# Converting float64 weights on Trainium2: the exponent handled by ScalarE's copy instead of a second VectorE mask

## The chip, the cores and the metric

The kernel runs on one core of one Trainium2 chip. Its time is the device time of one execution in microseconds (us), taken as the median of several runs. The engines are TensorE (PE in the profile; its weight loads are PEld), VectorE (DVE), ScalarE (ACT), GpSimd (POOL) and SyncE (SP), which issues the DMAs here.

## The reference

Attention with queries pooled in pairs, then two MLPs one after the other. The four MLP weight matrices arrive as float64, everything else as float32.

```python
# q, k, v: (4, 8, 1152, 64) float32; weights float64: w_in (512, 2048), w_out (2048, 512)
q_pool = q.reshape(B, H, S // 2, 2, D).mean(axis=3)
scores = q_pool @ k.T / sqrt(D)
attn = softmax(scores) @ v                 # per batch and head: 576 queries, 1152 keys
x = attn, heads side by side               # (2304, 512)
h = x @ moe_w_in;  x = maximum(0.01 * h, h) @ moe_w_out
h = x @ moe2_w_in; x = where(h > 0, h, exp(min(h, 0)) - 1) @ moe2_w_out
```

## The kernel before

All matrix products are done as sums of "high" and "low" float32r parts, so each operand is split: ScalarE or VectorE rounds the high part, GpSimd or VectorE subtracts it from the operand (`psplit`, L261 to L267). A source line that is such a helper's stands for many tiles, so the tile names matter: `wi` and `wo` are the split weights, `g` the split MLP activations, `pt` the split attention weights, `kn`, `qn`, `vn` the split inputs.

The work is cut into 16 attention pairs (a batch and two heads; nine query tiles each) and eight MLP passes (four batches, two layers). Attention of batch 1 runs beside the MLPs of batch 0, and so on; the MLPs of batch 3 run alone at the end. A pair ends with the normalising transposes L535. This document counts pairs from 0, so pairs 4 to 7 are batch 1.

The order of instructions on every engine is written out ahead of time. `Program.add` takes each operation with an engine, a planned cost and a rank; `Program.schedule` simulates all engines with those costs and sorts the operations by their planned start. Every engine, SyncE's DMA queue too, then takes its own list strictly in order. An edit of one operation therefore moves others, on all engines.

An MLP pass works through 16 slices of 128 hidden columns (`up`, L638; `down`, L676), in halves of 288 rows; one half of one slice is 12 matmuls in `up`, and a block of four slices for one output tile 12 in `down`. Layer 0's activation is finished on VectorE at L651, layer 1's at L659, and `down`'s partial sums are added at L689. On first use a weight slice is read as float64 and converted by `convert`, called from `load_w`; the float32 result is split at once and also stored to DRAM (L328), from where the later batches load it. `convert` runs 128 times over a chunk of 256 columns: 2 layers x 16 slices x 2 matrices x 2 chunks. Its buffers are rings of two (`CB`): `cr` holds the raw words, low and high interleaved, `ct` the word under construction, `cm` a second copy. A chunk's load (L290) can only start when the chunk two before it has left `cr`.

Per chunk, before: VectorE shifts the high word left by three and masks it (L293), VectorE puts the two top bits in (L296), ScalarE scales the low word (L299) and takes the magnitude of the high word (L301), GpSimd adds low to high (L303), and VectorE zeroes what is below float32's range (L305).

Of the kernel before, what the change touches and what calls it, by code (L numbers as in the profile page):

```python
# [9 lines left out]
F32 = mybir.dt.float32  # L10
F32R = mybir.dt.float32r
U32 = mybir.dt.uint32
ACTF = mybir.ActivationFunctionType
ALU = mybir.AluOpType
# [140 lines left out]
def kernel(  # L155
# [20 lines left out]
    V, A, G, PE = nc.vector, nc.scalar, nc.gpsimd, nc.tensor  # L176
# [10 lines left out]
    FT = DFF // 128  # L187
    QSCALE = 0.5 / float(D) ** 0.5
    HB = NQ // 2
    MIN_HI = 2.0 ** (112 - 127) * (1 + 2.0 ** -3)  # L190
    PTB = 4
    CW = 256
    CB = 2
# [47 lines left out]
    prog = Program()  # L241

    def sb(tag, shape, dt=F32, bufs=1):
        return prog.buf(tag, bufs, lambda: sp.tile(shape, dt, tag=tag, name=tag, bufs=bufs))
# [4 lines left out]
    def act(n, accum=False, sbuf=False):  # L249
        return 50 + 0.833 * n + (190 if accum else 0) + (43 if sbuf else 0)  # L250

    def dve(n, fast=False):
        return 66 + (0.52 if fast else 1.05) * n

    def pool(n):
        return 140 + 2.12 * n
# [14 lines left out]
    def convert(rank, dst, src):  # L271

        for n in range(0, 512, CW):
            r = sb("cr", [128, CW, 2], U32, CB)
            t = sb("ct", [128, CW], U32, CB)  # L280
            mag = sb("cm", [128, CW], F32, CB)

            def load(n=n, r=r):
                rv = r.ap.rearrange("p n t -> p (n t)")
                if len(src.shape) == 3:
                    k0, kn = n // src.shape[2], CW // src.shape[2]
                    rv, sv = rv.rearrange("p (c n) -> p c n", c=kn), src[:, k0:k0 + kn, :]
                else:
                    sv = src[:, n:n + CW]
                nc.sync.dma_start(out=rv, in_=sv.bitcast(U32))  # L290

            prog.add("SP", 60, rank - 1, load, w=[r])
            prog.add("DVE", dve(CW, True), rank, lambda r=r, t=t: V.tensor_scalar(  # L293
                out=t.ap, in0=r[:, :, 1], scalar1=3, scalar2=0x3FFFFFF8,
                op0=ALU.logical_shift_left, op1=ALU.bitwise_and), w=[t], r=[(r, 1)])
            prog.add("DVE", dve(CW), rank, lambda r=r, t=t: V.scalar_tensor_tensor(  # L296
                out=t.ap, in0=r[:, :, 1], scalar=0xC0000000, in1=t.ap,
                op0=ALU.bitwise_and, op1=ALU.bitwise_or), w=[t], r=[(r, 1), t])
            prog.add("ACT", act(CW, sbuf=True), rank, lambda r=r: A.activation(  # L299
                out=r[:, :, 0], in_=r[:, :, 0], func=ACTF.Copy, scale=2.0 ** -29), w=[(r, 0)], r=[(r, 0)])  # L300
            prog.add("ACT", act(CW, sbuf=True), rank, lambda r=r, mag=mag: A.activation(  # L301
                out=mag.ap, in_=r[:, :, 1].bitcast(F32), func=ACTF.Abs), w=[mag], r=[(r, 1)])
            prog.add("POOL", pool(CW), rank, lambda t=t, r=r: G.tensor_tensor(  # L303
                out=t.ap, in0=t.ap, in1=r[:, :, 0], op=ALU.add), w=[t], r=[t, (r, 0)])
            prog.add("DVE", dve(CW), rank, lambda n=n, t=t, mag=mag: V.scalar_tensor_tensor(  # L305
                out=dst[:, n:n + CW], in0=mag.ap, scalar=MIN_HI, in1=t.ap.bitcast(F32),
                op0=ALU.is_ge, op1=ALU.mult), w=[(dst, n)], r=[t, mag])

    kept = {}

    def load_w(rank, layer, w_in, w_out, f, mine):

        src = (w_in[:, f * 128:(f + 1) * 128].rearrange("(c p) f -> p c f", p=128),
               w_out[f * 128:(f + 1) * 128, :])
        rs = [mine("wr", [128, 512], F32, WRB, "p", PBUF) for _ in range(2)]
        for i, r in enumerate(rs):
            if w_in.dtype == F32:
                view = (lambda r=r: r.ap.rearrange("p (c n) -> p c n", c=DC)) if i == 0 else lambda r=r: r.ap
                prog.add("SP", 60, rank - 1.5, lambda i=i, view=view: nc.sync.dma_start(
                    out=view(), in_=src[i]), w=[r])  # L320
            elif (layer, f, i) in kept:
                kp = kept[layer, f, i]
                prog.add("SP", 60, rank - 1.5, lambda r=r, kp=kp: nc.sync.dma_start(
                    out=r.ap, in_=kp.ap), w=[r], r=[kp])
            else:
                convert(rank - CLEAD, r, src[i])
                kp = kept[layer, f, i] = Buf(lambda i=i: dram.tile([128, 512], F32, name=f"w{layer}_{f}_{i}"))
                prog.add("SP", 60, rank, lambda r=r, kp=kp: nc.sync.dma_start(out=kp.ap, in_=r.ap), w=[kp], r=[r])  # L328
        wi = mine("wi", [128, 2, DC, 128], F32R, WIB, "qT", KTB)
        wo = mine("wo", [128, 2, DM], F32R, WOB, "kT", KTB)  # L330
        psplit(rank - 0.5, WH, WL, lambda: wi[:, 0].rearrange("p c n -> p (c n)"),
               lambda: wi[:, 1].rearrange("p c n -> p (c n)"), lambda: rs[0].ap, 512, (wi, 0), [rs[0]])
        psplit(rank - 0.5, WH, WL, lambda: wo[:, 0], lambda: wo[:, 1], lambda: rs[1].ap, 512, (wo, 0), [rs[1]])
        return wi, wo
# [3 lines left out]
    for j in range(2):  # L338
        t = sp.tile([128, 2, 128], F32R, name=f"rem{j}")
# [400 lines left out]
    for b, layer, at, wide in PLAN:  # L740
        tags = [(u, size[u]) for u in ("h" * HBUFS + ("t" * TB + "s" * SBUFS if wide else ""))]
        w = ((moe_w_in, moe_w_out), (moe2_w_in, moe2_w_out))[layer]
# [35 lines left out]
```

## Time and profile before

| | |
|---|---|
| median of 3 runs | 1539.69 us (1537.06 to 1542.2) |
| profiled execution | span 1538.0 us from the first to the last instruction; no other time is recorded for it |
| PE busy | 1414.5 us, 92% |
| PEld busy | 1365.5 us, 89% |
| ACT busy | 1065.2 us, 69% |
| DVE busy | 1011.8 us, 66% |
| POOL busy | 829.8 us, 54% |
| mean granted TensorE clock | 0.988 |

Busy shares are means over stages that differ: the conversions all lie in the first 592 us, where VectorE is far busier than in the mean. They are therefore read stretch by stretch below.

### The profile page before, as it was taken

The numbers are of one execution on the slowest core, as the hardware profiler recorded it, in microseconds if no ns is written. First come the engines' busy times: TensorE is split into PE (matmuls) and PEld (weight loads), VectorE is DVE, ScalarE is ACT, GpSimd is POOL, SyncE is SP. The second block draws the span as 40 slices with busy tenths as digits, with TensorE's granted clock in tenths as the row PEclk, the third lists the DMA queues.
The fourth block names the chain that finished last, engine by engine and source line by source line (L and its number), as shares of the span: only waits on it lengthen the run. The fifth ranks groups of instructions, "written<-read, shape, count | busy, mean of one in ns | idle before, by whom it ended". The sixth has DMA issues, their size and how long they took to land.

```text
span 1538.0 us, 28928 instructions
## 1 busy us (share of the span) xinstructions
PE 1414.5 (92%) x10288; PEld 1365.5 (89%) x10288; DVE 1011.8 (66%) x2273; ACT 1065.2 (69%) x2901; POOL 829.8 (54%) x840
## 2 busy tenths in 40 slices
PE   5877889988888898999999999999999999999998
PEld 4777788888778887999999999899999998899998
DVE  6999888899998998556665556556665454123222
ACT  6998878776688787676668777676667773443553
POOL 5443355765766667354555555255555445466661
PEclk9999999999999999999999999999999999999999
DMA  4232123344434443222222222222222222323210
GB/s 147 91 115 87 40 77 121 122 130 129 127 119 139 132 143 118 76 75 69 69 68 86 79 78 64 71 71 61 76 71 64 56 63 63 106 77 89 70 55 32
DMA packets 82642, 135.59 MB, mean 88 GB/s; under 512 B 8512, under 2 KB 26944, under 8 KB 82496
## 3 DMA queue, kind: packets, MB, share of 16 engines
q1 hardware_dynamic: 82496, 133.73, 28.5%
q8 instruction: 81, 1.33, 0.4%
q14 instruction: 65, 0.53, 0.1%
HBM read 112.20 MB, written 21.50 MB: 87 GB/s over the span
## 4 chain that ended last, share of the span: by engine, by line
PE 63%; DVE 20%; ACT 7%; DMA 4%; issue 3%; POOL 2%; SPq 0%; ACTq 0%; POOLq 0%; DVEq 0%
PE h L676 16%; PE h L638 16%; PE s L452 8%; PE o L496 7%; PE t L475 5%; DVE m L457 3%; DVE ct L293 3%; DVE wr L305 3%; PE s L638 3%; PE s L676 3%; DVE ct L296 2%; DVE pt L267 2%; PE t L638 2%; PE t L373 2%; PE t L676 2%
## 5 line engine op out<-in xcount | busy, mean ns | idle before, releaser
L676 PE MATMUL h<-g,wo 128*128 128x288 f32 x2460 | 425.8, 303 | 16.7 <-DVE t L659 7.9
L638 PE MATMUL h<-xs,wi 128*128 128x288 f32 x2448 | 418.1, 305 | 23.3 <-DVE t L659 13.5
L638 PEld LDWEIGHTS h<-xs,wi 128*128 128x128 f32 x2448 | 351.8, 190 | 33.1 <-DVE t L659 19.0
L676 PEld LDWEIGHTS h<-g,wo 128*128 128x128 f32 x2460 | 356.9, 189 | 23.1 <-DVE t L659 9.9
L457 DVE TENSOR_REDUCE m<-s 128x1 f32<-128x384 f32 x432 | 231.8, 550 | 71.9 <-PE s L452 68.9
L261 ACT ACTIVATE pt<-t 128x384 fp32r<-128x384 f32 (+2 forms) x426 | 188.0, 456 | 117.3 <-PE t L475 109.1
L463 ACT ACTIVATE p<-s,m 128x384 f32<-128x384 f32 x432 | 249.1, 587 | 19.1 <-DVE m L459 18.7
L267 DVE TENSOR_TENSOR pt<-t,pt 128x384 fp32r<-128x384 f32 (+1 forms) x416 | 206.6, 508 | 74.0 <-ACT pt L261 72.6
L452 PE MATMUL s<-kT,qT 128*128 128x384 f32 x768 | 198.5, 356 | 25.7 <-ACT p L463 25.0
L267 POOL TENSOR_TENSOR g<-t,g 128x288 fp32r<-128x288 f32 x216 | 179.1, 833 | 67.6 <-ACT g L261 62.4
L267 POOL TENSOR_TENSOR wo<-wr,wo 128x512 fp32r<-128x512 f32 x112 | 145.9, 1307 | 108.2 <-ACT wo L261 106.3
L496 PE MATMUL o<-pt,vn 128*128 128x256 f32 (+1 forms) x1152 | 192.1, 302 | 5.4 <-DVE pt L267 3.5
L475 PE MATMUL t<-ident,p 128*128 128x128 f32 x1116 | 181.8, 277 | 12.3 <-DVE pt L267 11.3
L267 POOL TENSOR_TENSOR wi<-wr,wi 128x512 fp32r<-128x512 f32 x110 | 144.0, 1310 | 62.9 <-ACT wi L261 48.9
L496 PEld LDWEIGHTS o<-pt,vn 128*128 128x128 f32 x1152 | 165.1, 190 | 10.4 <-DVE pt L267 10.0
L475 PEld LDWEIGHTS t<-ident,p 128*128 128x128 f32 x1116 | 139.8, 142 | 21.9 <-DVE pt L267 11.8
L452 PEld LDWEIGHTS s<-kT,qT 128*128 128x128 f32 x768 | 126.2, 193 | 32.9 <-ACT p L463 31.8
L303 POOL TENSOR_TENSOR ct<-ct,cr 128x256 uint32<-128x256 uint32 x128 | 98.8, 774 | 95.5 <-DVE ct L296 33.8
L267 POOL TENSOR_TENSOR vn<-raw,vn 128x576 fp32r<-128x576 f32 x32 | 46.3, 1448 | 174.5 <-ACT vn L261 174.5
L261 ACT ACTIVATE g<-t 128x288 fp32r<-128x288 f32 x216 | 95.9, 446 | 44.1 <-DVE t L659 26.2
L689 DVE TENSOR_TENSOR acc<-h,acc 128x288 f32<-128x288 f32 x158 | 71.0, 452 | 66.2 <-PE h L676 64.9
L261 ACT ACTIVATE wo<-wr 128x512 fp32r<-128x512 f32 x112 | 70.5, 630 | 46.3 <-PE h L676 33.5
(150 smaller groups left out, 2228.4 us busy)
## 6 DMA issues: line engine op xcount, KB each, us to landing
wr<-w SPq DMA_DIRECT2D x172, 256.0 KB, 2.7
cr<-in_moe_w_in_dram SPq DMA_DIRECT2D x64, 256.0 KB, 2.8
cr<-in_moe_w_out_dram SPq DMA_DIRECT2D x64, 256.0 KB, 2.7
w<-wr SPq DMA_DIRECT2D x64, 256.0 KB, 2.4
raw<-in_k_dram SPq DMA_DIRECT2D x32, 288.0 KB, 3.0
raw<-in_v_dram SPq DMA_DIRECT2D x32, 288.0 KB, 3.1
raw<-in_q_dram SPq DMA_DIRECT2D x32, 256.0 KB, 2.9
p<-w SPq DMA_DIRECT2D x20, 256.0 KB, 2.6
```

The lines of the kernel that those rows point to most:

```text
L261: prog.add("ACT", act(n, sbuf=not psum), rank, lambda: A.activation(out=hi(), in_=src(), func=ACTF.Copy), w=[w], r=r)
L267: lambda: eng.tensor_tensor(out=lo(), in0=src(), in1=f32(hi()), op=ALU.subtract),
L293: prog.add("DVE", dve(CW, True), rank, lambda r=r, t=t: V.tensor_scalar(out=t.ap, in0=r[:, :, 1], scalar1=3, scalar2=0x3FFFFFF8, op0=ALU.l ...
L303: prog.add("POOL", pool(CW), rank, lambda t=t, r=r: G.tensor_tensor(out=t.ap, in0=t.ap, in1=r[:, :, 0], op=ALU.add), w=[t], r=[t, (r, 0)])
L452: PE.matmul(out=st[:, 0:384], lhsT=qa(a), rhs=kT[:, 384 * c:384 * c + 384], start=(i == 0), stop=(i == len(seq) - 1))
L457: prog.add("DVE", dve(384), rank - LR, lambda st=st, c=c: V.tensor_reduce(out=m[:, c:c + 1], in_=st[:, 0:384], axis=AX.X, op=ALU.max), w=[ ...
L463: prog.add("ACT", act(384, True), rank - LE, lambda c=c: A.activation(out=p[:, 384 * c:384 * c + 384], in_=banks[c][:, 0:384], func=ACTF.E ...
L475: PE.transpose(out=t[:, i, :], in_=p[:, (3 * c + i) * 128:(3 * c + i + 1) * 128], identity=ident)
L496: PE.matmul(out=o[:, 0:n], lhsT=vn[:, c, :], rhs=pt[th][:, a, c % 3, :], start=(c == 3 * ORDER[0] and a == 0), stop=(c == 3 * ORDER[2] + 2 ...
L638: PE.matmul(out=h[:, 0:HB], lhsT=wi[:, a, c, :], rhs=xs[c][:, e, cols], start=(c == 0 and a == 0 and e == 0), stop=(c == DC - 1 and a == 1))
L676: PE.matmul(out=y[:, 0:HB], lhsT=w[f][1][:, a, d * 128:(d + 1) * 128], rhs=g[f][:, e, cols], start=(f % FC == 0 and a == 0 and e == 0), st ...
L689: prog.add("DVE", dve(HB), rank - HURRY, lambda y=y, a_=a_, cols=cols: V.tensor_tensor(out=a_[:, cols], in0=y[:, 0:HB], in1=a_[:, cols], o ...
```

## The change

ScalarE copies the high word, read as a float32, with a scale of 2^-112, which rebases the exponent in the arithmetic and sends what is too small to zero, into `cm`. VectorE shifts that copy left by three (one operation, contiguous input), GpSimd adds the low part as before, and VectorE joins the sign bit of the copy to the sum. The second VectorE mask (L296) and the magnitude copy (L301) are gone; the comparison at L305 becomes a bitwise join. Per chunk there are two ScalarE, two VectorE and one GpSimd instruction where there were two, three and one. The shift now reads what ScalarE wrote, where L293 read the loaded word itself.

```diff
-            mag = sb("cm", [128, CW], F32, CB)
+            g = sb("cm", [128, CW], F32, CB)
...
-            prog.add("DVE", dve(CW, True), rank, lambda r=r, t=t: V.tensor_scalar(
-                out=t.ap, in0=r[:, :, 1], scalar1=3, scalar2=0x3FFFFFF8,
-                op0=ALU.logical_shift_left, op1=ALU.bitwise_and), w=[t], r=[(r, 1)])
-            prog.add("DVE", dve(CW), rank, lambda r=r, t=t: V.scalar_tensor_tensor(
-                out=t.ap, in0=r[:, :, 1], scalar=0xC0000000, in1=t.ap,
-                op0=ALU.bitwise_and, op1=ALU.bitwise_or), w=[t], r=[(r, 1), t])
+            prog.add("ACT", act(CW, sbuf=True), rank, lambda r=r, g=g: A.activation(
+                out=g.ap, in_=r[:, :, 1].bitcast(F32), func=ACTF.Copy, scale=REBIAS), w=[g], r=[(r, 1)])
             prog.add("ACT", act(CW, sbuf=True), rank, lambda r=r: A.activation(
                 out=r[:, :, 0], in_=r[:, :, 0], func=ACTF.Copy, scale=2.0 ** -29), w=[(r, 0)], r=[(r, 0)])
-            prog.add("ACT", act(CW, sbuf=True), rank, lambda r=r, mag=mag: A.activation(
-                out=mag.ap, in_=r[:, :, 1].bitcast(F32), func=ACTF.Abs), w=[mag], r=[(r, 1)])
+            prog.add("DVE", dve(CW, True), rank, lambda g=g, t=t: V.tensor_scalar(
+                out=t.ap, in0=g.ap.bitcast(U32), scalar1=3, scalar2=None,
+                op0=ALU.logical_shift_left), w=[t], r=[g])
             prog.add("POOL", pool(CW), rank, lambda t=t, r=r: G.tensor_tensor(
                 out=t.ap, in0=t.ap, in1=r[:, :, 0], op=ALU.add), w=[t], r=[t, (r, 0)])
-            prog.add("DVE", dve(CW), rank, lambda n=n, t=t, mag=mag: V.scalar_tensor_tensor(
-                out=dst[:, n:n + CW], in0=mag.ap, scalar=MIN_HI, in1=t.ap.bitcast(F32),
-                op0=ALU.is_ge, op1=ALU.mult), w=[(dst, n)], r=[t, mag])
+            prog.add("DVE", dve(CW), rank, lambda n=n, t=t, g=g: V.scalar_tensor_tensor(
+                out=dst[:, n:n + CW].bitcast(U32), in0=g.ap.bitcast(U32), scalar=0x80000000, in1=t.ap,
+                op0=ALU.bitwise_and, op1=ALU.bitwise_or), w=[(dst, n)], r=[t, g])
```

In the changed kernel the ScalarE copies are L293 (high) and L295 (low), the shift is L297, the GpSimd add L300, the join L302; all lines behind are three lower (L457 becomes L454).

VectorE's order in pair 5, around the pair's remainder tile (`pt` of 3x64), before. L457 is the row maximum of the scores, L651 layer 0's activation:

```order
L267 TENSOR_TENSOR pt<-t,pt 128x3x64
L457 TENSOR_REDUCE m<-s 128x1
L305 SCALAR_TENSOR_TENSOR wr<-cm,ct 128x256
L267 TENSOR_TENSOR pt<-t,pt 128x3x64
L293 TENSOR_SCALAR ct<-cr 128x256
L296 SCALAR_TENSOR_TENSOR ct<-cr,ct 128x256
L651 TENSOR_TENSOR t_4545<-h,t_4545 128x288
L457 TENSOR_REDUCE m<-s 128x1
L305 SCALAR_TENSOR_TENSOR wr<-cm,ct 128x256
```

The same place in the changed kernel (L454 is the row maximum, L648 the activation):

```order
L297 TENSOR_SCALAR ct<-cm 128x256
L454 TENSOR_REDUCE m<-s 128x1
L297 TENSOR_SCALAR ct<-cm 128x256
L456 TENSOR_REDUCE m<-m 128x1
L267 TENSOR_TENSOR pt<-t,pt 128x3x64 x3
L648 TENSOR_TENSOR t_4503<-h,t_4503 128x288
L454 TENSOR_REDUCE m<-s 128x1
L648 TENSOR_TENSOR t_4514<-h,t_4514 128x288
L454 TENSOR_REDUCE m<-s 128x1 x2
L302 SCALAR_TENSOR_TENSOR wr<-cm,ct 128x256 x2
```

Two chunks now go through side by side: two shifts, other work, two joins; a row maximum stands behind each shift, where before it stood behind the activation or the join.

ScalarE's order there, before (L261 with `pt`, `g`, `wi`: high parts; L463 the softmax exponential, L649 the activation's first half):

```order
L261 ACTIVATE pt<-t 128x3x64
L649 ACTIVATE t_4491<-h 128x288
L463 ACTIVATE p,sum<-s,m 128x384 x2
L261 ACTIVATE g<-t_4491 128x288
L261 ACTIVATE pt<-t 128x3x64
L299 ACTIVATE cr<-cr 128x256
L301 ACTIVATE cm<-cr 128x256
L649 ACTIVATE t_4545<-h 128x288
```

And in the changed kernel (L646 is the activation, L460 the exponential):

```order
L646 ACTIVATE t_4428<-h 128x288
L261 ACTIVATE pt<-t 128x3x64 x2
L293 ACTIVATE cm<-cr 128x256
L295 ACTIVATE cr<-cr 128x256
L261 ACTIVATE g<-t_4428 128x288
L293 ACTIVATE cm<-cr 128x256
L295 ACTIVATE cr<-cr 128x256
L261 ACTIVATE wo<-wr 128x512
L460 ACTIVATE p,sum<-s,m 128x384 x3
```

The copy of the high word now comes first of a chunk's two, and in these rows two chunks stand close together with one split of `g` between them.

## Rows read from the trace of the kernel before

**Rows 1.** The page, part 1: busy time and share of the span.

```profile
PE 1414.5 (92%) x10288; PEld 1365.5 (89%) x10288; DVE 1011.8 (66%) x2273; ACT 1065.2 (69%) x2901; POOL 829.8 (54%) x840
```

**Rows 2.** Windows, busy us (instructions) of each engine; boundaries are the pairs' L535.

```profile
core 0: us, PE busy (x) PEld busy (x) DVE busy (x) ACT busy (x) POOL busy (x), PEclk, DMA share, GB/s
65.00:112.00 47.00, 38.04 (x262) 34.49 (x261) 43.87 (x109) 42.75 (x123) 21.24 (x22) 0.96 0.32 100
...
158.00:201.00 43.00, 35.65 (x258) 32.57 (x257) 36.03 (x88) 36.41 (x105) 12.04 (x13) 1.00 0.14 42
201.00:270.00 69.00, 63.24 (x445) 59.06 (x443) 60.25 (x141) 56.31 (x162) 37.39 (x39) 0.98 0.33 103
...
270.00:589.00 319.00, 278.97 (x1968) 260.61 (x1966) 300.70 (x629) 243.11 (x681) 212.59 (x223) 0.99 0.42 131
...
589.00:679.00 90.00, 81.82 (x595) 79.51 (x594) 55.59 (x124) 62.27 (x167) 43.51 (x43) 0.96 0.28 84
...
679.00:933.00 254.00, 253.49 (x1924) 252.41 (x1923) 151.44 (x352) 180.43 (x491) 133.65 (x130) 1.00 0.25 72
...
933.00:1027.00 94.00, 89.02 (x648) 86.66 (x647) 55.06 (x121) 63.61 (x172) 47.06 (x46) 0.96 0.25 77
...
1450.00:1500.00 50.00, 50.00 (x379) 50.00 (x378) 12.35 (x29) 26.90 (x65) 32.53 (x32) 1.00 0.20 61
```

**Rows 3.** The same windows, L638 alone, then L676 alone: PE, PEld.

```profile
679.00:933.00 254.00, 98.55 (x576) 81.96 (x576) 1.00 0.25 72
...
679.00:933.00 254.00, 101.73 (x585) 85.37 (x585) 1.00 0.25 72
```

**Rows 4.** The chain that ended last, in 270 to 589 us, by line.

```profile
by line: DVE ct L293 10.5%; DVE wr L305 10.4%; DVE ct L296 9.8%; issue 7.9%; DVE m L457 7.1%; DVE pt L267 5.5%; DMA cr<-in_moe_w_out_dram 5.3%; PE h L638 4.4%; DMA cr<-in_moe_w_in_dram 3.3%; DVE acc L689 3.1%; ACT p L463 3.0%; POOL ct L303 
```

**Rows 5.** Groups of VectorE by line, 270 to 589 us: busy us, mean ns | idle before.

```profile
L305 DVE SCALAR_TENSOR_TENSOR wr<-cm,ct 128x256 f32<-128x256 f32 x90 | 63.6, 710 | 1.3 <-POOL ct L303 1.2
L296 DVE SCALAR_TENSOR_TENSOR ct<-cr,ct 128x256 uint32<-128x256 uint32 x90 | 59.7, 665 | 0.7
L293 DVE TENSOR_SCALAR ct<-cr 128x256 uint32<-128x256 uint32 x90 | 51.2, 571 | 1.6 <-DMA cr<-in_moe_w_out_dram 0.9 <-DMA cr<-in_moe_w_in_dram 0.6
...
L689 DVE TENSOR_TENSOR acc<-h,acc 128x288 f32<-128x288 f32 x40 | 17.8, 447 | 2.0 <-PE h L676 1.9
```

**Rows 6.** Tile `ct`, whole run: ns min/median/max, then idle until (us, times).

```profile
L293 DVE TENSOR_SCALAR ct<-cr x128: 272/294/1524, 7.8 to 587.7; 128x256 uint32<-128x256 uint32 x128
L296 DVE SCALAR_TENSOR_TENSOR ct<-cr,ct x128: 403/425/1659, 9.4 to 589.2; 128x256 uint32<-128x256 uint32 x128
L303 POOL TENSOR_TENSOR ct<-ct,cr x128: 729/747/1034, 11.9 to 589.7; 128x256 uint32<-128x256 uint32 x128
L305 DVE SCALAR_TENSOR_TENSOR wr<-cm,ct x128: 402/416/1678, 12.7 to 591.4; 128x256 f32<-128x256 f32 x128
...
  DVE ct L296: 33.8, 26
...
  ACT cr L299: 6.2, 5
```

**Rows 7.** Timeline at 286 us: start us, duration us, instruction.

```profile
286.68 1.49 POOL L267 TENSOR_TENSOR wo<-wr,wo 128x512 fp32r<-128x512 f32 x1
...
286.94 1.38 DVE L293 TENSOR_SCALAR ct<-cr 128x256 uint32<-128x256 uint32 x1
...
288.13 0.85 POOL L267 TENSOR_TENSOR g<-t,g 128x288 fp32r<-128x288 f32 x1
...
288.36 0.91 DVE L296 SCALAR_TENSOR_TENSOR ct<-cr,ct 128x256 uint32<-128x256 uint32 x1
```

**Rows 8.** Tile `cr`, whole run: ScalarE's two copies.

```profile
L299 ACT ACTIVATE cr<-cr x128: 418/438/489, 7.8 to 587.4; 128x256 uint32<-128x256 uint32 x128
...
L301 ACT ACTIVATE cm<-cr x128: 414/428/478, 8.1 to 588.0; 128x256 f32<-128x256 f32 x128
```

**Rows 9.** Tile `qs`: a contiguous VectorE tensor_scalar of the same size.

```profile
L399 DVE TENSOR_SCALAR qs<-qs x32: 229/286/1494, 8.6 to 1141.4; 128x256 f32<-128x256 f32 x32
```

**Rows 10.** Waits of the DMA queue, 201 to 589 us: us, times, longest.

```profile
SPq L290 <- POOL ct L303: 156.4, 101, 5.2
```

**Rows 11.** Waits of VectorE, 270 to 589 us: us, times, longest.

```profile
DVE t L651 <- ACT t L649: 4.4, 4, 2.7
```

More of the change, by code (lines that the diff above doesn't have):

```diff
@@ L189 @@
     HB = NQ // 2
-    MIN_HI = 2.0 ** (112 - 127) * (1 + 2.0 ** -3)
+    REBIAS = 2.0 ** -112
     PTB = 4
```

## Prediction

> **What bounds the kernel now.** I read the page's busy shares first [rows 1]: TensorE is busy 92% of the span, so at first sight it bounds everything and VectorE, at 66%, nothing. Then I cut the span at the ends of the attention pairs [rows 2]. From 679 to 933 us (pairs 9 to 11, no conversions) TensorE is busy 253.5 of 254 us: bound by TensorE, and nothing on VectorE can help. From 270 to 589 us (pairs 5 to 7, where 90 of the 128 chunks are converted) it is the other way round: VectorE is busy 300.7 of 319 us, 94.3%, TensorE 279, ScalarE 243, GpSimd 213. There VectorE is the bound, and the chain of waits of that stretch says so: L293, L305 and L296 are its three longest lines, 30.7% of it together [rows 4].
>
> How much could come back at most? In 1450 to 1500 us only MLP matmuls run, 379 in 50 us without a gap [rows 2]: 0.132 us each. Pairs 9 to 11 hold 576 + 585 = 1161 of them [rows 3], 153 us, which leaves 33.6 us of TensorE for the attention of one pair. The order of before puts 1197 MLP matmuls into pairs 5 to 7, so TensorE alone would need 3 x 33.6 + 1197 x 0.132 = 259 us. They take 319. The conversions cost 60 us here; that is the room.
>
> **The change, part by part.** *The mask L296 goes.* Alone it takes 0.41 us (shortest 403 ns, median 425); in pairs 5 to 7 its mean is 665 ns [rows 5, 6]. The difference is waiting, and the timeline shows for what [rows 7]: GpSimd subtracts for `wo` from 286.68 to 288.17; the shift that VectorE starts at 286.94 lasts until 288.32, 1.38 us instead of 0.28. The mask behind it starts at 288.36, under the next GpSimd instruction, and takes 0.91. So the relief per chunk lies between 0.41 us (the waiting passes to the next instruction in line) and 0.665 us (it leaves too): 37 to 60 us in 90 chunks. I take 0.41, because the two instructions that stay, shift and join, meet the same GpSimd. [...]
>
> *The shift* reads contiguous words instead of every second one. L399, contiguous and as large, has 229 ns at its shortest and 286 at its median, against 272 and 294 for L293 [rows 6, 9]: between 0 and 43 ns less, at most 4 us in 90 chunks. I take 0, as the medians agree. [...]
>
> *The join* is a two-input bitwise instruction like L296, 403 ns at its shortest, for a comparison of 402 [rows 6]: nothing. *ScalarE* does two copies per chunk as before; a scaled copy (median 438) for a magnitude (428) [rows 8] is 10 ns, about 1 us over 128 chunks on an engine 76% busy in this stretch: nothing while it stays under VectorE, and 1 us if it does not. *GpSimd's* add is untouched (747 ns).
>
> *A denser stretch waits more.* Shift and join stand 571 - 272 and 710 - 402 ns above their shortest, 0.61 us a chunk, 55 us in 90 chunks [rows 5, 6]. GpSimd is busy 67% of the stretch; in some 282 us it would be 73%, and waits that grow in proportion add 5 us.
>
> *Matmuls move.* Counted in the new order, pairs 4 to 8 hold 273, 378, 351, 351 and 354 MLP matmuls, where they held 201, 414, 414, 369 and 309. Behind pair 8 the two orders hold the same counts. So pairs 5 to 7 lose 117 matmuls, hence about 10 VectorE instructions like L689 at 0.447 us [rows 5], 4.4 us.
>
> The sum for pairs 5 to 7: VectorE 300.7 - 37 - 4.4 + 5 = 264.3 us. At the 94.3% that it reached before, 280 us; TensorE's floor is now 243 (100.8 + 1080 x 0.132). Gain 39 us. Pair 4 gets 72 matmuls more: TensorE needs 33.6 + 36.0 = 69.6 us, at the 92% it had there 76, against 69 now: 6 to 7 us lost, I take 6. Pair 8: 33.6 + 46.7 us and the first output stage, which by pair 12 (94 us with 375 matmuls, 83.1 of work) costs 11: 91 against 90, 1 lost. The first 201 us: a pair with conversions takes 47 us, the one without 43 [rows 2]; a third of those 4 us, in two or three pairs, is 3 us gained. From pair 9 on nothing moves. Net 39 - 6 - 1 + 3 = 35 us. The profiled execution has a span of 1538.0 us, 0.1% under the median of 1539.69; taken off the median: **1505 us**.
>
> **What the change adds as a wait.** The shift needs ScalarE's copy of the high word, where L293 needed only the load. Behind a shift that waits, VectorE holds row maxima and `pt` low parts, for which ScalarE's exponential and TensorE's second product wait. In the sum this wait is zero, because ScalarE was the earlier of the two: GpSimd's add found itself held by VectorE's half 26 times for 33.8 us and by ScalarE's low word 5 times for 6.2 [rows 6]. If that cover is gone, each 0.1 us per shift costs 106 x 0.1 / 0.943 = 11 us in pairs 4 to 7.
>
> **The rivals.** *TensorE becomes the bound.* The mask's waiting leaves with it: VectorE 300.7 - 60 - 4 = 237, at 94.3% 251 us, 8 above TensorE's floor. Gain 68, pairs 4 and 8 lose 2, the start gains 4: 1470 us, and 1492 where only half the waiting leaves. For it: GpSimd idles in this stretch, so not every instruction meets it. Against: so dense a stretch has three engines at about 240 us, with no slack to hide a wait.
>
> *The ring of two holds the pace.* The DMA queue stood 101 times for 156 us until GpSimd had emptied a `cr` buffer [rows 10], so a chunk's turn (load, convert, free) is closed: 319/90 x 2 = 7.1 us. In that turn the mask's 0.665 us goes and ScalarE's 0.43 comes in ahead of the shift: 0.23 less per turn, 0.12 per chunk, 11 us. With the moved matmuls about 1534. For it: the closed ring. Against: load, copy, shift and add alone are far below 7 us, the rest is queueing behind other work, and that shrinks with VectorE's load. Between this and my sum lies 1520 to 1534.
>
> *No change.* The same ring, with another 0.2 us of waiting for ScalarE: the turn stays at 7.1 us, the pairs as they were: 1540.
>
> *Slower: the shift waits for ScalarE.* ScalarE takes its list in order too, and where its copy stands behind a split of `g` that itself waits for VectorE, both stand. The mechanism decides from 0.41 us of wait per shift on, where it eats the mask. At 0.6 us: 106 x 0.19 / 0.943 = 21 us lost, with the moved matmuls about 1565. For it: where VectorE did wait for ScalarE in this stretch, at L651, it was 1.1 us each time [rows 11]. Against: that was 4 times in 319 us.
>
> **How the numbers follow.** My sum (1492 to 1520) has 0.44, TensorE as the bound (1470 to 1492) 0.17, the ring (1520 to 1534) 0.22, no change 0.08, slower 0.09. A measurement tells some 0.3%, 5 us, from no change. Faster is 0.44 + 0.17 + 0.22 = 0.83, same 0.08, slower 0.09. The range 1478 to 1540 leaves out the slower case, half of no change, and the lower third of the TensorE case: 0.19.
>
> **What would show it.** Pairs 5 to 7 (their L532 to L532) near 280 us with VectorE still above 90%; pair 4 longer by about 6; everything behind pair 8 as long as before. The shift's mean near 0.6 us shows that the waiting stayed; a mean under 0.45 speaks for TensorE as the bound. Idle VectorE in front of L297, released by ScalarE's L293, with more than 10 us in total, would make the prediction wrong on the high side; so would a DMA queue that waits for L300 while VectorE falls below 85%.

## The result, and the profile after

The changed kernel takes 1502.74 us (median of 4 runs, 1500.38 to 1503.84) against 1538.7 us for the kernel before (1537.06 to 1542.2, 4 runs): a ratio of 0.9762, 95% interval 0.9746 to 0.9779. The profiled execution has a span of 1500.4 us. The page's busy shares, which answer to [rows 1], show VectorE 57 us less busy, TensorE 15 us less (its mean granted clock is 0.994 for 0.988), and ScalarE and GpSimd nearly as before:

```profile
PE 1399.9 (93%) x10288; PEld 1357.1 (90%) x10288; DVE 955.2 (64%) x2145; ACT 1064.0 (71%) x2901; POOL 826.0 (55%) x840
```

The windows between the pairs' ends answer to [rows 2] (us, then PE, PEld, DVE, ACT, POOL busy):

```profile
62.00:108.00 46.00, 37.63 (x261) 34.55 (x260) 40.38 (x102) 42.48 (x123) 21.54 (x23) 0.96 0.32 103
...
153.00:196.00 43.00, 35.67 (x258) 32.56 (x257) 35.97 (x87) 36.46 (x105) 12.00 (x12) 1.00 0.14 42
196.00:271.00 75.00, 70.77 (x517) 67.06 (x514) 65.33 (x141) 63.44 (x182) 47.85 (x51) 1.00 0.35 116
...
271.00:550.50 279.50, 255.84 (x1852) 242.89 (x1851) 246.71 (x523) 232.41 (x653) 197.96 (x211) 1.00 0.45 146
...
550.50:644.00 93.50, 86.68 (x642) 83.55 (x641) 58.44 (x125) 65.22 (x175) 45.00 (x44) 1.00 0.24 75
...
644.00:898.00 254.00, 253.49 (x1926) 252.51 (x1925) 151.61 (x352) 180.76 (x491) 133.59 (x130) 1.00 0.24 72
```

The time came from where it was looked for. Differences of the window lengths, after less before:

| stretch | before | after | difference | forecast |
|---|---|---|---|---|
| start to the end of pair 3 | 201 | 196 | -5 | -3 |
| pair 4 | 69 | 75 | +6 | +6 |
| pairs 5 to 7 | 319 | 279.5 | -39.5 | -39 |
| pair 8 | 90 | 93.5 | +3.5 | +1 |
| behind pair 8 | 859 | 856.4 | -2.6 | 0 |
| sum | 1538.0 | 1500.4 | -37.6 | -35 |

The windows of before are cut at whole microseconds, so a difference can be off by 1 us. Of the 2.6 us behind pair 8, two are pair 12: 92 us for 94, with TensorE busy 87.0 us for 89.0 at a mean granted clock of 1.00, where it was 0.96.

The lengths agree; what fills them does not. In pairs 5 to 7 VectorE is busy 246.7 us, not 264, and that is 88% of the stretch, not 94.3%. No engine is above 92% there any more. VectorE's groups of this stretch, beside [rows 5] (line, instruction, count, busy us, mean ns, idle before):

```profile
L302 DVE SCALAR_TENSOR_TENSOR wr<-cm,ct 128x256 uint32<-128x256 uint32 x88 | 71.3, 813 | 5.4 <-POOL ct L300 5.1
L297 DVE TENSOR_SCALAR ct<-cm 128x256 uint32<-128x256 uint32 x88 | 46.8, 535 | 7.8 <-ACT cm L293 7.3
```

Shift and join together take 1.348 us a chunk, where shift, mask and last step took 0.571 + 0.665 + 0.710 = 1.946. The difference, 0.598 us, is far above the mask's unblocked 0.41: the 0.25 us that the mask stood waiting went with it, and 0.07 came back at shift and join. The trace of before shows why. Sorted by whether a GpSimd instruction is under way when they start, 44 of the 90 masks in pairs 5 to 7 start beside none and take 426 ns at most; the other 46 take 907 ns on average. Shift and join part in the same way, and they start beside GpSimd about as often as before: 47 and 52 times in 90, then 48 and 56 in 88.

The shift itself is no faster from contiguous words (tile `ct`, ns min/median/max; before 272/294 [rows 6]):

```profile
L297 DVE TENSOR_SCALAR ct<-cm x128: 272/296/1426, 8.2 to 542.3; 128x256 uint32<-128x256 uint32 x128
L300 POOL TENSOR_TENSOR ct<-ct,cr x128: 725/747/1027, 10.5 to 543.1; 128x256 uint32<-128x256 uint32 x128
L302 DVE SCALAR_TENSOR_TENSOR wr<-cm,ct x128: 405/476/1655, 11.2 to 544.4; 128x256 uint32<-128x256 uint32 x128
```

What VectorE does in the other 33 us of the stretch (before it idled 18 of 319) is in its waits, 271 to 550.5 us (us, times, longest):

```profile
DVE ct L297 <- ACT cm L293: 7.3, 13, 1.5
DVE m L454 <- PE s L449: 5.3, 7, 1.2
DVE wr L302 <- POOL ct L300: 5.1, 11, 0.6
DVE pt L267 <- ACT pt L261: 4.3, 11, 0.7
```

No wait is large; these four are 22 of the 33 us, and VectorE now waits a little for each of the other three. The chain of waits of the stretch still has conversion lines at its head, but 18.7% in L302 and L297 for 30.7% in three lines before [rows 4]:

```profile
by line: DVE wr L302 12.2%; issue 7.7%; DMA cr<-in_moe_w_in_dram 7.1%; PE h L635 7.0%; DVE ct L297 6.5%; DVE m L454 5.4%; PE h L673 5.4%; POOL ct L300 5.0%; DVE pt L267 4.6%; DMA cr<-in_moe_w_out_dram 4.3%; ACT cm L293 3.5%; PE s L449 2.6%;
```

### The profile page after: what moved, and what is told of

Read it like the earlier page. It is cut to its first block, busy times and chain, and to the rows that moved or that the text cites. A ratio compares the mean times of both kernels' runs of the same rounds, so it can differ in the third digit from the quotient of the medians.

```text
span 1500.4 us, 28730 instructions
## 1 busy us (share of the span) xinstructions
PE 1399.9 (93%) x10288; PEld 1357.1 (90%) x10288; DVE 955.2 (64%) x2145; ACT 1064.0 (71%) x2901; POOL 826.0 (55%) x840
## 4 chain that ended last, share of the span: by engine, by line
PE 67%; DVE 16%; ACT 8%; DMA 4%; issue 3%; POOL 2%; SPq 0%; ACTq 0%; POOLq 0%; DVEq 0%
PE h L673 17%; PE h L635 17%; PE s L449 8%; PE o L493 7%; PE t L472 5%; DVE wr L302 3%; PE s L635 3%; PE s L673 3%; DVE m L454 3%; PE t L370 2%; DVE pt L267 2%; PE t L635 2%; ACT pt L261 2%; DMA cr<-in_moe_w_in_dram 2%; PE t L673 2%
## 5 line engine op out<-in xcount | busy, mean ns | idle before, releaser
L673 PE MATMUL h<-g,wo 128*128 128x288 f32 x2460 | 420.8, 301 | 13.5 <-DVE t L656 9.9
L635 PE MATMUL h<-xs,wi 128*128 128x288 f32 x2448 | 413.8, 303 | 16.2 <-DVE t L656 6.5
L454 DVE TENSOR_REDUCE m<-s 128x1 f32<-128x384 f32 x432 | 232.8, 551 | 79.8 <-PE s L449 75.3
L261 ACT ACTIVATE pt<-t 128x384 fp32r<-128x384 f32 (+2 forms) x426 | 188.2, 457 | 112.6 <-PE t L472 103.9
L460 ACT ACTIVATE p<-s,m 128x384 f32<-128x384 f32 x432 | 249.4, 588 | 12.9 <-DVE m L456 12.6
L300 POOL TENSOR_TENSOR ct<-ct,cr 128x256 uint32<-128x256 uint32 x128 | 96.8, 761 | 84.0 <-ACT cr L295 25.1
L261 ACT ACTIVATE g<-t 128x288 fp32r<-128x288 f32 x216 | 95.9, 447 | 28.4 <-DVE t L656 16.7
L261 ACT ACTIVATE wo<-wr 128x512 fp32r<-128x512 f32 x112 | 70.4, 631 | 44.1 <-PE h L673 34.3
```

What stands on the lines that cost most here:

```text
L261: prog.add("ACT", act(n, sbuf=not psum), rank, lambda: A.activation(out=hi(), in_=src(), func=ACTF.Copy), w=[w], r=r)
L454: prog.add("DVE", dve(384), rank - LR, lambda st=st, c=c: V.tensor_reduce(out=m[:, c:c + 1], in_=st[:, 0:384], axis=AX.X, op=ALU.max), w=[ ...
L460: prog.add("ACT", act(384, True), rank - LE, lambda c=c: A.activation(out=p[:, 384 * c:384 * c + 384], in_=banks[c][:, 0:384], func=ACTF.E ...
L635: PE.matmul(out=h[:, 0:HB], lhsT=wi[:, a, c, :], rhs=xs[c][:, e, cols], start=(c == 0 and a == 0 and e == 0), stop=(c == DC - 1 and a == 1))
L673: PE.matmul(out=y[:, 0:HB], lhsT=w[f][1][:, a, d * 128:(d + 1) * 128], rhs=g[f][:, e, cols], start=(f % FC == 0 and a == 0 and e == 0), st ...
```

## The experiments

All twelve ran beside the kernel before on their chip; ratios are to that kernel with 95% intervals, and the changed kernel's is 0.9762. Line numbers of a variant shift by a few where it has more lines; the tile names tell which instruction it is. The kernel before has medians of 1538.7 to 1542.1 us in the four sets of runs, so a difference between medians of two sets carries about 3 us.

### The order or the instructions?

The new instructions came with a new order on every engine. Two runs take them apart. One plans the shift at what shift and mask cost together, which was to bring the order near the old one; the other keeps the old instructions and plans the mask at nothing.

```diff
-            prog.add("DVE", dve(CW, True), rank, lambda g=g, t=t: V.tensor_scalar(
+            prog.add("DVE", dve(CW, True) + dve(CW), rank, lambda g=g, t=t: V.tensor_scalar(
```

> The changed instructions, but the shift is planned at the cost that shift and mask had together (199 + 335 ns), so that the planner writes an order close to the old one. My theory (VectorE's own time in pairs 4 to 7 is what is saved, the order matters little): 1496 to 1511 us, near the changed kernel's 1502.7. Rival (the new order, with two chunks side by side and 72 matmuls moved into pair 4, brings the gain): most of it is lost, 1525 to 1540.

Measured: 1497.1 us (1496.65 to 1501.96), ratio 0.9727 (0.9706 to 0.9747). The gain is all there in this order. But the order is a third one, not the old one. By the windows of the traces, pairs 4 to 8 hold 199, 390, 438, 366 and 315 MLP matmuls before, 258, 389, 356, 356 and 354 in the changed kernel, and 276, 362, 416, 381 and 277 here: pair 4 has taken over even more than in the changed kernel. Nor are two chunks side by side new: before, 58 of the 128 shifts are followed by another shift ahead of the next join, in the changed kernel 45. So this run shows that the gain survives another order; what parts order and instructions is the next run.

```diff
-            prog.add("DVE", dve(CW), rank, lambda r=r, t=t: V.scalar_tensor_tensor(
+            prog.add("DVE", 1, rank, lambda r=r, t=t: V.scalar_tensor_tensor(
```

> The old instructions, but the mask is planned at 1 ns, so that the order is written as if it were not there. My theory: no gain, 1533 to 1552 us, VectorE still above 92% busy in the pairs that convert. Rival (the order): 1503 to 1515, as in the changed kernel.

Measured: 1549.96 us (1545.81 to 1551.35), ratio 1.0060 (1.0041 to 1.0078): 0.6% slower than before, although pair 4 holds 252 MLP matmuls, nearly as in the changed kernel. In its pairs 5 to 7 VectorE is busy 282.00 of 310.40 us, 91%, not above 92 as expected. An order written as if the mask were not there gains nothing; the instruction has to go.

### What an instruction on VectorE costs here: two inputs or one, inside the chunk's turn or outside

Four runs put one extra VectorE instruction into every chunk of the changed kernel, in its own order (the planner does not see it). Where it is not held up it takes the same 0.40 to 0.43 us each time. It was to differ in two ways: whether it has two SBUF inputs, like the mask, or one (a row maximum); and whether GpSimd's add, which frees the raw buffer, has to wait for it (inside the turn) or not. In each, shift and extra are one operation of the plan; the diffs show only the two calls.

Two inputs, inside the turn, behind the shift:

```diff
                 V.tensor_scalar(out=t.ap, in0=g.ap.bitcast(U32), scalar1=3, scalar2=None,
                                 op0=ALU.logical_shift_left)
+                V.scalar_tensor_tensor(out=t.ap, in0=g.ap.bitcast(U32), scalar=0, in1=t.ap,
+                                       op0=ALU.bitwise_and, op1=ALU.bitwise_or)
```

> The changed kernel in its own order, with a VectorE instruction of the mask's form (two SBUF inputs, 128x256) put back behind each shift, where its result changes nothing; the planner does not see it. My theory: 106 chunks in pairs 4 to 7 at 0.41 us over a share of 0.9 to 0.94, less a few us of slack, so 35 to 46 us more: 1538 to 1549. If the waiting comes and goes with the instruction (0.665 us a chunk): 70 us more, 1565 to 1580. If the order made the gain: under 10 us more.

One input, outside the turn, behind the shift (`junk` is one float32 column):

```diff
                 V.tensor_scalar(out=t.ap, in0=g.ap.bitcast(U32), scalar1=3, scalar2=None,
                                 op0=ALU.logical_shift_left)
+                V.tensor_reduce(out=junk, in_=g.ap, axis=AX.X, op=ALU.max)
```

> The changed kernel in its own order with another extra VectorE instruction behind each shift: a row maximum over the 128x256 copy into a column that nobody reads, one SBUF input, which by the rows of L457 does not wait for GpSimd; some 0.40 us each. GpSimd's add does not depend on it. My theory (VectorE's time is what counts): as much as in the run with two inputs, less what that one waits for GpSimd: 32 to 44 us more, 1535 to 1547. Rival (the ring of two raw buffers sets the pace): the extra work lies outside the turn, at most 12 us more, below 1515. Rival (contention with GpSimd is what counts): under half of the loss with two inputs.

Two inputs, outside the turn, behind the shift:

```diff
                 V.tensor_scalar(out=t.ap, in0=g.ap.bitcast(U32), scalar1=3, scalar2=None,
                                 op0=ALU.logical_shift_left)
+                V.scalar_tensor_tensor(out=g.ap.bitcast(U32), in0=g.ap.bitcast(U32), scalar=0,
+                                       in1=g.ap.bitcast(U32), op0=ALU.bitwise_and, op1=ALU.bitwise_or)
```

> The changed kernel with an extra VectorE instruction of two SBUF inputs behind each shift as in the run with two inputs, but it rewrites the copy cm with itself, so GpSimd's add does not depend on it: outside the turn of the raw ring, the same length. The first four runs left this open: the extra with two inputs, which the add waits for, cost 54 us, the one with one input, which the add does not wait for, 19. Theory turn (what lengthens load, copy, shift, add, free is paid): as the run with one input, 1517 to 1528 us. Theory contention (what takes the second SBUF input is paid, waiting for GpSimd and holding it): as the run with two inputs, 1545 to 1560.

One input, inside the turn, in front of the shift:

```diff
+                V.tensor_reduce(out=junk, in_=g.ap, axis=AX.X, op=ALU.max)
                 V.tensor_scalar(out=t.ap, in0=g.ap.bitcast(U32), scalar1=3, scalar2=None,
                                 op0=ALU.logical_shift_left)
```

> The changed kernel with the row maximum of 0.41 us in front of each shift instead of behind it: one SBUF input, no contention, but inside the turn, since the shift and so the add come 0.41 us later. Theory turn: as the run with two inputs, 1545 to 1558 us. Theory contention: as the run with the maximum behind the shift, 1517 to 1528.

Measured, median and what it adds to the changed kernel's 1502.7:

| | inside the turn | outside the turn |
|---|---|---|
| two SBUF inputs | 1556.47 us, +54; ratio 1.0101 (1.0085 to 1.0117) | 1545.48 us, +43; ratio 1.0030 (1.0013 to 1.0047) |
| one SBUF input | 1519.25 us, +17; ratio 0.9874 (0.9839 to 0.9909) | 1521.35 us, +19; ratio 0.9876 (0.9858 to 0.9894) |

The two-input form costs 24 to 37 us more than the other, the turn 11 at the most and nothing with one input. By the ratios the four prices are 52, 41, 17 and 18 us, the same picture. My expectation that both extras would cost about the same fell with the first pair of runs; the two-input run itself, 1556, lies between my range (1538 to 1549) and that of the waiting that comes and goes with the instruction (1565 to 1580). The turn of the ring fell with the second pair. In pairs 5 to 7, by the windows of each run:

| pairs 5 to 7 | length, us | VectorE busy, us |
|---|---|---|
| changed kernel | 279.5 | 246.7 |
| one input, outside | 294.2 | 270.6 |
| one input, inside | 295.2 | 270.9 |
| two inputs, outside | 312.4 | 288.7 |
| two inputs, inside | 322.9 | 295.7 |

VectorE's groups in that stretch show part of the reason (columns as above). Two inputs, inside; L300 is the extra:

```profile
L306 DVE SCALAR_TENSOR_TENSOR wr<-cm,ct 128x256 uint32<-128x256 uint32 x89 | 74.1, 836 | 5.1 <-POOL ct L304 4.0 <-POOL wo L267 0.8
L300 DVE SCALAR_TENSOR_TENSOR ct<-cm,ct 128x256 uint32<-128x256 uint32 x88 | 50.6, 575 | 3.0
L298 DVE TENSOR_SCALAR ct<-cm 128x256 uint32<-128x256 uint32 x88 | 45.6, 518 | 3.7 <-ACT cm L293 3.5
```

One input, outside; L301 is the extra:

```profile
L306 DVE SCALAR_TENSOR_TENSOR wr<-cm,ct 128x256 uint32<-128x256 uint32 x88 | 68.7, 787 | 1.2 <-DMA w<-wr 0.7 <-POOL ct L304 0.5
L299 DVE TENSOR_SCALAR ct<-cm 128x256 uint32<-128x256 uint32 x88 | 45.6, 518 | 5.2 <-ACT cm L294 4.9
L301 DVE TENSOR_REDUCE junk<-cm 128x1 f32<-128x256 f32 x88 | 35.8, 407 | 0.0
```

The row maximum takes 407 ns on average, its unblocked length. Tile `junk` over the whole run:

```profile
L301 DVE TENSOR_REDUCE junk<-cm x128: 402/406/414, 9.2 to 560.4; 128x1 f32<-128x256 f32 x128
```

The kernel's own row maximum is not held up either: L457 before took 535 to 560 ns in all 432 cases, 165 of them started beside a GpSimd instruction. The extra maximum also writes only one column, where the two-input extra writes 256. That a write to SBUF alone does not bring the waiting, an instruction of the kernel itself shows: L648 reads one operand from PSUM and one from SBUF and writes 128x288 to SBUF. In the changed kernel it is never held up, although 70 of the 105 start beside a GpSimd instruction:

```profile
L648 DVE TENSOR_TENSOR t<-h,t x105: 438/457/459, 204.1 to 1369.3; 128x288 f32<-128x288 f32 x105
```

Nor does it take two SBUF inputs to be held up: the shift has one, and in pairs 5 to 7 of the changed kernel the 48 that start beside a GpSimd instruction take 743 ns on average, the other 40 take 297 at most. What in an instruction's form decides it, the runs do not show.

The maximum's 35.8 us raise VectorE's busy time by only 23.9 (270.6 - 246.7). The other instructions take only 2.7 us less in sum; the rest is overlap. In these traces the records of two VectorE instructions overlap by some 80 ns where the second does not need the first, and so the maximum overlaps the shift in all 88 chunks. The two-input extra takes 575 ns, and VectorE's busy time rises by 49.0 us, nearly its whole 50.6. Both two-input extras write a tile that the shift in front of them has read or written, and they start 34 ns behind its end, in all 88 chunks. That is 0.11 us a chunk which has nothing to do with GpSimd, by my estimate up to 15 of the 24 to 37 us over 128 chunks. The extra's own waiting is of the same size, 0.15 us a chunk inside the turn and 0.09 outside (575 and 516 ns for some 425 unblocked). The four runs do not part the two in the price.

Outside the turn, with two inputs (groups of the stretch; L300 the extra, L304 GpSimd's add, 765 ns on average in the changed kernel):

```profile
L300 DVE SCALAR_TENSOR_TENSOR cm<-cm 128x256 uint32<-128x256 uint32 x88 | 45.4, 516 | 3.0
...
L304 POOL TENSOR_TENSOR ct<-ct,cr 128x256 uint32<-128x256 uint32 x88 | 80.5, 916 | 59.8 <-DVE ct L298 18.9 <-ACT cr L295 18.4 <-ACT pt L261 6.8
```

Here it is GpSimd that is held up. The same run's timeline at 302 us (start, duration, instruction):

```profile
302.14 0.28 DVE L298 TENSOR_SCALAR ct<-cm 128x256 uint32<-128x256 uint32 x1
...
302.45 0.42 DVE L300 SCALAR_TENSOR_TENSOR cm<-cm 128x256 uint32<-128x256 uint32 x1
302.55 0.94 POOL L304 TENSOR_TENSOR ct<-ct,cr 128x256 uint32<-128x256 uint32 x1 [1.45 <-ACT pt L261]
```

The add starts 0.1 us behind the extra and takes 0.94 us for 0.75: each of the two engines is held up by the other. Over the whole run (the changed kernel's add has 725/747/1027):

```profile
L304 POOL TENSOR_TENSOR ct<-ct,cr x128: 729/928/984, 10.5 to 583.8; 128x256 uint32<-128x256 uint32 x128
```

One input inside the turn (L299 the extra) is as cheap as outside; the shift behind it takes 484 ns for 535, with as many meetings (50 of 88) but shorter ones:

```profile
L300 DVE TENSOR_SCALAR ct<-cm 128x256 uint32<-128x256 uint32 x88 | 42.6, 484 | 0.0
L299 DVE TENSOR_REDUCE junk<-cm 128x1 f32<-128x256 f32 x88 | 36.0, 409 | 5.7 <-ACT cm L294 5.3
```

### GpSimd's add taken away

If waiting for GpSimd is what shift and join take beyond their shortest, less GpSimd must shorten them. This run keeps the order and leaves out the add; its weights lack the low mantissa bits.

```diff
-            prog.add("POOL", pool(CW), rank, lambda t=t, r=r: G.tensor_tensor(
-                out=t.ap, in0=t.ap, in1=r[:, :, 0], op=ALU.add), w=[t], r=[t, (r, 0)])
+            prog.add("POOL", pool(CW), rank, lambda: None, w=[t], r=[t, (r, 0)])
```

> The changed kernel in its own order without GpSimd's add of the low word: the weights then lack their low mantissa bits, all else is there. [...] Rival (GpSimd's add costs VectorE nothing): 1496 to 1506.

Measured: 1483.22 us (1481.67 to 1486.24), ratio 0.9615 (0.9564 to 0.9666): 13 us below the range in which the add costs VectorE nothing. Pairs 5 to 7 take 261.9 us, with VectorE busy 222.0; its groups there:

```profile
L301 DVE SCALAR_TENSOR_TENSOR wr<-cm,ct 128x256 uint32<-128x256 uint32 x88 | 51.8, 596 | 0.0
L297 DVE TENSOR_SCALAR ct<-cm 128x256 uint32<-128x256 uint32 x88 | 43.3, 496 | 8.8 <-ACT cm L293 8.0
```

No VectorE instruction was taken away, and VectorE's busy time fell by 25 us; shift and join lost 0.26 us a chunk (1.348 to 1.092), 22 us of it. The shift starts beside a GpSimd instruction 36 times for 48, the join 30 times for 56. The stretch lost 18. The join no longer depends on GpSimd either, so the 5 us that it idled for it are gone as well, and a raw buffer comes free without the add; the run does not part these.

### The ring and the order of ScalarE's copies

A third conversion buffer needs room, so one of six buffers of split output weights goes; the second run has only that edit.

```diff
-    CB = 2
+    CB = 3
...
-    WOB = 6
+    WOB = 5
```

> The changed kernel with three conversion buffers of each kind instead of two; to make room, one buffer of split output weights less (five for six). To be read against the run with only that buffer less. Theory turn: a third buffer takes the turn off the path, 12 to 30 us less than that run. My theory of the prediction (VectorE's time): within 6 us of it.

> The changed kernel with five buffers of split output weights instead of six and nothing else: the control for the ring of three. Every theory: 1500 to 1515 us.

Measured: 1499.31 us (1498.4 to 1500.8), ratio 0.9735 (0.9710 to 0.9760), and 1498.42 us (1493.66 to 1502.16), ratio 0.9727 (0.9695 to 0.9759) for the control. The control missed its range (1500 to 1515) by 1.6 us on the fast side. The third buffer brings nothing, although the DMA queue waits half as long for GpSimd to free one; its wait in pairs 5 to 7, control first, then three buffers (before [rows 10]):

```profile
SPq L290 <- POOL ct L300: 157.3, 85, 5.2
```

```profile
SPq L290 <- POOL ct L300: 82.0, 67, 2.9
```

ScalarE does wait for the loads: L293 8.0 us in pairs 5 to 7 of the changed kernel. But a buffer that is free earlier shortens nothing, so the ring does not set the pace.

Last, ScalarE's two copies of a chunk in the other order, low word first:

```diff
-            prog.add("ACT", act(CW, sbuf=True), rank, lambda r=r, g=g: A.activation(
-                out=g.ap, in_=r[:, :, 1].bitcast(F32), func=ACTF.Copy, scale=REBIAS), w=[g], r=[(r, 1)])
             prog.add("ACT", act(CW, sbuf=True), rank, lambda r=r: A.activation(
                 out=r[:, :, 0], in_=r[:, :, 0], func=ACTF.Copy, scale=2.0 ** -29), w=[(r, 0)], r=[(r, 0)])
+            prog.add("ACT", act(CW, sbuf=True), rank, lambda r=r, g=g: A.activation(
+                out=g.ap, in_=r[:, :, 1].bitcast(F32), func=ACTF.Copy, scale=REBIAS), w=[g], r=[(r, 1)])
```

> The changed kernel with ScalarE's two copies of a chunk in the other order, low word first: the copy that the shift needs comes one instruction, 0.43 us, later. If the shift's wait for ScalarE is the price that the prediction put at 11 us per 0.1 us of it (nothing covers it): 1525 us and more. If VectorE seldom gets there first and the turn of the ring has slack: within 8 us of the changed kernel's 1502.7, 1497 to 1511.

Measured: 1498.37 us (1495.96 to 1500.89), ratio 0.9712 (0.9669 to 0.9756). In pairs 5 to 7 the shift waits for ScalarE twice as long as in the changed kernel (7.3 us), and nothing is lost: VectorE's busy time there falls from 247 to 230 us, of 274.3. Some 5 of these 17 us are four chunks that fall into pair 8 (84 for 88); the rest is mainly shift and join, 1.199 us a chunk for 1.348. VectorE's wait, then its groups:

```profile
DVE ct L297 <- ACT cm L295: 14.1, 22, 1.6
```

```profile
L302 DVE SCALAR_TENSOR_TENSOR wr<-cm,ct 128x256 uint32<-128x256 uint32 x84 | 62.7, 755 | 6.3 <-POOL ct L300 5.9
L297 DVE TENSOR_SCALAR ct<-cm 128x256 uint32<-128x256 uint32 x84 | 36.8, 444 | 14.3 <-ACT cm L295 14.1
```

The shift takes 444 ns for 535. It starts beside a GpSimd instruction 41 times in 84 (changed kernel: 48 in 88) and then takes 611 ns on average for 743. So it meets GpSimd nearly as often and for a shorter time; why shorter is not shown, as the order of other work moved too.

### Can the planner do better?

Two more variants of the plan: shift and join at what they were measured to take, and the shift at 534 ns together with five output-weight buffers.

```diff
-            prog.add("DVE", dve(CW, True), rank, lambda g=g, t=t: V.tensor_scalar(
+            prog.add("DVE", 535, rank, lambda g=g, t=t: V.tensor_scalar(
...
-            prog.add("DVE", dve(CW), rank, lambda n=n, t=t, g=g: V.scalar_tensor_tensor(
+            prog.add("DVE", 813, rank, lambda n=n, t=t, g=g: V.scalar_tensor_tensor(
```

> The changed kernel, planned with what shift and join were measured to take in pairs 5 to 7, 535 and 813 ns, for 199 and 335. The run with the shift alone planned at 534 gave 1497.1. If the gain there came from a truer plan: 1485 to 1497. If it came from the accident of another order: 1495 to 1515.

```diff
-            prog.add("DVE", dve(CW, True), rank, lambda g=g, t=t: V.tensor_scalar(
+            prog.add("DVE", dve(CW, True) + dve(CW), rank, lambda g=g, t=t: V.tensor_scalar(
...
-    WOB = 6
+    WOB = 5
```

> The shift planned at 534 ns together with five buffers of split output weights for six: the two variants that gave 1497.1 and 1498.4. If what they gain is the same slack in pairs 4 to 8, it does not add: 1490 to 1503. If they are separate gains: 1484 to 1493.

Measured: 1504.26 us (1502.88 to 1504.35), ratio 0.9748 (0.9707 to 0.9790), and 1499.66 us (1496.5 to 1501.58), ratio 0.9719 (0.9675 to 0.9762). A truer plan was not a faster one here, and the two small gains do not add. (The first of the two has a lower granted clock, 0.986 to 0.990 in its four runs against 0.991 to 0.996 for the changed kernel, and 0.95 in its pairs 5 to 7; how much of its time that is, is open.) The six orders of the changed instructions tried here (the changed kernel, the two with their plan altered alone, five buffers, both together, low word first) lie between 1497.1 and 1504.3 us, where the runs of one kernel alone spread by up to 8.5 us. The lowest ratio, 0.9712 (low word first), has an interval that overlaps the changed kernel's; the shift planned at 534 ns, 0.9727, lies 0.36% lower, and the two intervals just meet: a version that is clearly better did not come out.

## Why the prediction was right, and where it was not

**What bounds it, and where.** Right. All but a few us came from pairs 4 to 8 and the start; pairs 9 to 11 still take 254 us with TensorE busy 253.5. An instruction of the mask's form put back into the changed order loses all of the gain, and an order written as if the mask were free brings none.

**The relief per chunk** is the step that failed: "between 0.41 us (the waiting passes to the next instruction in line) and 0.665 us (it leaves too) ... I take 0.41". Measured, 0.598 us left a chunk, 54 us in 90 chunks and not 37. The waiting belongs to the pair of instructions that meet, one of VectorE that GpSimd can hold up and one of GpSimd. Take such a VectorE instruction away and its meetings go with it, the mask's 46 of 90; put one back and they return (575 ns on average, 424 at the shortest). The row maximum of one input is not held up at all (402 to 414 ns). Both sides of a meeting can be held up: GpSimd's add took 0.94 us behind the two-input extra. But not for the other's whole length: the shift at 286.94 us ends 0.15 us behind GpSimd's instruction [rows 7], where 0.28 is its own length, and the add 0.62 us behind the extra, with 0.75. That the waiting stays because shift and join meet the same GpSimd was my own step, and wrong.

**The share that VectorE can reach** failed in the other direction. I divided by the 94.3% of before; after, it is 88%. Had VectorE kept 94.3%, its 246.7 us would have made 262, towards the 251 of the rival with TensorE as the bound. The two errors, 18 us each, cancelled: 264.3/0.943 = 280 as forecast, 246.7/0.883 = 279.5 as measured. That the forecast of the stretch was right to 1 us is therefore partly luck, and the range, not the number, is what the working supported. Why 88%: with TensorE at 92%, VectorE at 88% and ScalarE at 83%, each in fixed order, VectorE waits a little for all three, as its rows of waits show; that this is the whole reason is argued. The four runs with an extra instruction trace a curve: VectorE's busy time rises by 24 us and the stretch by 15; by 42 and 49 us, and the stretch by 33 and 43. In these four runs the stretch follows VectorE about us for us above some 270 us of it. On the other side of the changed kernel it hardly does. Pairs 4 to 8 of the changed kernel, then with the low word first:

```profile
195.70:643.80 448.10, 413.38 (x3005) 393.59 (x3004) 370.60 (x787) 361.17 (x1009) 290.81 (x305) 1.00 0.39 126
```

```profile
196.30:642.00 445.70, 414.40 (x3006) 395.13 (x3004) 354.06 (x787) 360.42 (x1009) 290.34 (x305) 1.00 0.40 127
```

VectorE is busy 16.5 us less in the second, and the pairs take 2.4 us less, with TensorE busy 92 and 93%. So in the changed kernel VectorE alone no longer sets the length of these pairs, and the share was not a property of VectorE that could be carried over.

**The shift from contiguous words, the join, the copies, a denser stretch.** The shift's median is 296 ns for 294: zero, as taken. The shortest is 272 ns as before, and 229 in the run with three conversion buffers. The join's shortest is 405 for 402: zero. Shift and join together rose from 1.281 to 1.348 us, 6 us in 90 chunks; 5 were taken. But they did not rise in proportion: the shift fell from 571 to 535 ns and the join rose from 710 to 813. The shift's mean lies between the two signs named for it, near 0.6 and under 0.45 us, and decides for neither.

**Matmuls that move.** Pair 4 was forecast 6 us longer and is; pair 8 1 and is 3.5. Pair 4 took over 59 matmuls by the windows of the traces, where 72 were counted in the order. Behind pair 8 nothing was to move, and 2.6 us did, 2 of them in pair 12, where the granted clock was 1.00 for 0.96.

**The added wait for ScalarE** was put at zero. It exists, 7.3 us in 13 waits in pairs 5 to 7, below the 10 us named as the mark. The mark itself and the price of 11 us per 0.1 us found no support: with 11.4 us of it (the shift planned at 534 ns) and 14.1 us (low word first) the kernel was no slower than the changed one. In these runs other work moved too.

**The rivals.** The ring of two is refuted by the third buffer and by the maximum inside the turn. Slower, through ScalarE, did not come, and the run with the later copy leaves its price without support. TensorE as the bound was right about the waiting and, at 280 us against its 251, wrong about the length.

## What to carry to other kernels

Where VectorE and GpSimd both work in SBUF, cost a VectorE instruction by what the trace shows of its form beside GpSimd, and by whether it must wait for the instruction in front of it. Here an instruction of some 0.42 us with two SBUF inputs, which started only behind the end of the shift in front of it, cost 43 to 54 us over 128 uses, and a row maximum of 0.41 us, which GpSimd did not hold up, 17 to 19. A busy share of VectorE contains the waiting for GpSimd (in pairs 5 to 7 of before, some 78 of 301 us by the means and shortest times of three instructions), so compare an instruction's mean with its shortest before calling the engine full. And when the bound of a stretch is relieved, do not carry its old share over: here the next engines were close by, and some of the time came back as small waits for each of them (VectorE idle 33 us of pairs 5 to 7, 18 before).

## What was not expected of the hardware

A row maximum over 128x256 in SBUF took 402 to 414 ns in all 128 cases behind the shift, whatever GpSimd did (busy 198 of 294 us there), and 409 ns on average over 88 cases in front of it. Behind the shift it raised VectorE's busy time by only two thirds of its length (23.9 of 35.8 us), as its record overlaps its neighbours' by some 80 ns. The two-input extras, which need the shift in front of them, instead start 34 ns behind its end. The waiting between the two engines lengthens GpSimd's instruction as well: its add had a median of 928 ns in the run where a two-input VectorE instruction stands right behind the shift that releases it, against 747.
